# The opening of a fused window-attention and maxout kernel: another order for chunk 0, weights in other pieces, two stores later in a queue

## The chip, the cores and the metric

The kernel runs on one core of a Trainium2 chip. A core has TensorE (matrix products into PSUM, eight banks), VectorE, ScalarE, GpSimd and SyncE, each with an instruction stream of its own, and 16 DMA engines that they share. In the profile's rows these are PE (products) and PEld (their weight loads), DVE, ACT, POOL and SP. The metric is the time of one execution in device microseconds, the median of several runs; lower is better.

## The reference

```
scores = q k^T / 8, of q, k, v: (4 batches, 8 heads, 768 tokens, 64)
keep   = first 4 positions (sinks), or 0 <= token - position < 128
x      = softmax(scores where kept) v, heads side by side: (3072, 512)
h      = max(max(x w1, x w2), x w3)         w1, w2, w3: (512, 768)
out    = h w_out                            w_out: (768, 512), out float32
```

All inputs are float32; the kernel computes its products in bfloat16 with float32 sums.

## The kernel before

The 3072 tokens are cut into 12 chunks of 256, three for each batch, and everything is written out by hand: the kernel is under a manual schedule, each engine takes its instructions in the order of the program's lines, and semaphores make it wait where data or a buffer is not there yet. So the list of calls from line 454 to 660 is the order of each engine's work for chunks 0 to 3; a loop (line 661) does the rest. The change touches that list.

What the calls do, chunk `ci` and (for attention) pair of heads `p` from 0 to 3:

- `load` (line 76) fetches q, k or v of a chunk, 512 KB of float32, on SyncE's queue, whole or in two halves. A `gate` is a one-element write of GpSimd into the target, which holds the load back: `after(wi, c)` (434) copies from column `c` of weight `wi`, and so waits for the piece of the weight that holds the column; `pool_gate` (440) writes a zero.
- `cast_qk` (95) and `cast_v` (104) cast to bfloat16, in halves and quarters, on the engine named. `turn` (109) and `turn2` (129) transpose half of the heads (`g` 0: pairs 0 and 1; `g` 1: pairs 2 and 3) by four TensorE transposes and a copy out of PSUM into `kT` or `qT`. `turn_dma` (150) does it by a DMA transpose for later chunks.
- `premask` (251) begins the score tiles of a pair by a product that writes the mask; `score` (259) adds the scores of the pair. A pair without `premask` is masked after the exponential by `mask` (289) on VectorE. `expo` (282) is two exponentials on ScalarE. `sink_k`, `sink_score`, `sink_v` and `av_open` (224 to 335) are the same for the four sink positions, which chunks 1 and 2 of a batch need. `av` (339) is values times weights, the division and the write into `x_sb`.
- `xpose` (364) transposes the x of half a chunk. `ffn_h(ci, fp, wi)` (383) is a third of the columns (`fp` 0 to 2, 256 each) of x times weight `wi` (0 to 2): eight products of 128 x 256. For weight 0 ScalarE copies the result to `h_sb`, for the others VectorE takes the maximum with what is there. `ffn_y` (406) is half of a chunk's output, six products; `store` (426) writes a chunk out from SyncE's queue.
- `load_w` (234) fetches columns of a weight by a casting DMA issued from GpSimd's queue, float32 to bfloat16, `load_wo` (242) the output weight in two halves.
- `warm` (172) issues products of a zero tile that nothing uses.
- PSUM banks come from a list in order of release (`bank`, `give`, lines 57 to 65): whoever takes a bank waits for its last reader.

The ring of `kT`, `qT`, `vb` has four chunks; raw q, k, v and their casts have two buffers each, y and x two, xT and h three.

Of the kernel before, what the change touches and what calls it, by code (L numbers as in the profile page):

```python
# [16 lines left out]
def kernel(  # L17
# [31 lines left out]
    with tc.manual_schedule():  # L49
# [289 lines left out]
        def av(ci, p):  # L339
# [16 lines left out]
            if p == 0:  # L356
                xs[ci] = work.tile([128, 2, NP, 2, D], BF16, tag="x", bufs=2, name="x_sb")
# [25 lines left out]
        def ffn_h(ci, fp, wi, cuts=1):  # L383
# [12 lines left out]
            if wi == 0:  # L396
                nc.scalar.copy(dst, hp)  # L397
# [8 lines left out]
        def ffn_y(ci, t, eng=None):  # L406
            if t == 0:
                ys[ci] = work.tile([128, 2, d_model], F32, tag="y", bufs=2, name="y_sb")
# [7 lines left out]
        def ffn_y_part(ci, t, c0, c1, eng):  # L416
            if t == 0 and c0 == 0:
                ys[ci] = work.tile([128, 2, d_model], F32, tag="y", bufs=2, name="y_sb")
# [39 lines left out]
        warm(2)  # L458
# [5 lines left out]
        warm(7)  # L464
        cast_qk(0, 'k', 0, nc.vector)
        cast_qk(0, 'k', 1, nc.gpsimd)
        cast_qk(0, 'q', 0, nc.gpsimd)
        premask(0, (0,))
        cast_qk(0, 'q', 1, nc.scalar)
        turn(0, 'k', 0, nc.vector)  # L470
        turn(0, 'k', 1, nc.scalar)
        turn(0, 'q', 1, nc.scalar)
        premask(0, (3,))
        load(1, 'k')
        turn(0, 'q', 0, nc.vector)
        score(0, (0,))
        premask(0, (2,))
        cast_v(0, 0, 0, nc.vector)
        cast_v(0, 1, 0, nc.gpsimd)
        cast_v(0, 1, 1, nc.vector)  # L480
        cast_qk(1, 'k', 0, nc.vector)
        premask(0, (1,))
        load(1, 'q')
        load_w(0, 512, 768)
        load_w(0, 0, 512)
        score(0, (1,))
        score(0, (2,))
        expo(0, 0)
        warm(3)
        sink_k(0)  # L490
        cast_v(0, 0, 1, nc.vector)
        expo(0, 1)
        load_w(1, 512, 768)
        turn2(1, 'k', 0, nc.vector)
        expo(0, 2)
        cast_qk(1, 'k', 1, nc.scalar)
        av_open(0)
        cast_qk(1, 'q', 0, nc.scalar)
        av(0, 0)
        score(0, (3,))  # L500
        sink_v(0)
        cast_qk(1, 'q', 1, nc.gpsimd)
        load_w(1, 0, 512)
        av(0, 1)
        load(1, 'v')
        expo(0, 3)
        turn(1, 'k', 1, nc.scalar)
        turn(1, 'q', 1, nc.vector)
        turn2(1, 'q', 0, nc.vector)
        cast_v(1, 0, 0, nc.gpsimd)  # L510
        cast_v(1, 1, 1, nc.gpsimd)
        cast_v(1, 1, 0, nc.gpsimd)
        cast_v(1, 0, 1, nc.gpsimd)
        premask(1, (0,))
        av(0, 3)
        load(2, 'k', part=0, parts=2, gate=after(0, 300))
        score(1, (0,))
        score(1, (2,))
        av(0, 2)
        load_w(2, 0, 256)  # L520
        load(2, 'k', part=1, parts=2)
        premask(1, (3,))
        score(1, (3,))
        expo(1, 0)
        xpose(0, 0, nc.vector)
# [3 lines left out]
        xpose(0, 1, nc.vector)  # L529
        load_w(2, 256, 512)  # L530
        sink_score(1)
        load_w(2, 512, 768)
        premask(1, (1,))
        score(1, (1,))
        av_open(1)
        cast_qk(2, 'k', 1, nc.gpsimd)
        mask(1, 2)
        expo(1, 3)
        load(2, 'v', gate=after(0, 300))
        expo(1, 1)  # L540
        av(1, 0)
        load(3, 'q', gate=after(2))
        ffn_h(0, 2, 0)
        av(1, 2)
        av(1, 3)
        av(1, 1)
        cast_qk(2, 'k', 0, nc.scalar)
        load(3, 'k')
        ffn_h(0, 0, 0)
        ffn_h(0, 2, 1)  # L550
        ffn_h(0, 1, 0)
        xpose(1, 0, nc.vector)
        xpose(1, 1, nc.vector)
        ffn_h(0, 1, 1)
        ffn_h(1, 0, 0)
        ffn_h(0, 0, 1)
        load_wo()
        factors(msk0, addm0)
        ffn_h(1, 2, 0)
        turn(2, 'k', 0, nc.vector)  # L560
        ffn_h(1, 1, 0)
# [48 lines left out]
        turn(3, 'k', 1, nc.scalar)  # L610
        load(5, 'k', gate=after(0, 300))
        av(2, 1)
        cast_qk(4, 'q', 1, nc.vector)
        turn(3, 'k', 0, nc.scalar)
        ffn_y(1, 0)
        cast_v(3, 1, 1, nc.gpsimd)
        score(3, (1,))
# [198 lines left out]
```

## Time and profile before

| | |
|---|---|
| median of three runs | 178.46 us (178.2 to 179.15) |
| profiled execution | 178.04 us |
| its span in the profile | 176.3 us |
| granted TensorE clock | 0.997 |
| TensorE busy | 169.8 us |
| DMA | 34.90 MB, 31.33 of them on the hardware queue (SyncE), 3.15 on the software queue (GpSimd, weights; counted as written) |

The profile is of one execution. All times are from the start of its span. A row of the timeline has start, length, engine, line of the code, operation and what it writes and reads, and in brackets how long the engine was idle before it and what ended that. A TensorE row's length has the tail of its pipeline in it, so costs are taken from start to start. A row of the DMA view has a queue, its packets, megabytes and share of 16 engines in the stretch asked for (q1 is SyncE's queue, q0 GpSimd's), or a kind of transfer, its size and the time from issue to landing.

### The profile page before, as it was taken

How to read it: one execution, taken by the hardware profiler on the slowest of the kernel's cores; microseconds unless marked ns; L12 is line 12 of the kernel's file. 1: busy time of each engine (PE TensorE's matmuls, PEld its weight loads, DVE VectorE, ACT ScalarE, POOL GpSimd, SP SyncE). 2: the span in 40 equal slices, each digit the busy share in tenths (PEclk: the TensorE clock that was granted, in tenths of full speed). 3: DMA queues.
4: the chain of work that ended last, by engine and by line, in shares of the span. 5: the costliest groups of instructions: out<-in, count | busy, mean ns of one | idle time of the engine just before them, and what ended most of it. 6: DMA issues, size and time to landing. Idle time of an engine off the chain costs nothing.

```text
span 176.3 us, 4635 instructions
## 1 busy us (share of the span) xinstructions
PE 169.8 (96%) x1864; PEld 127.0 (72%) x1877; DVE 120.7 (68%) x262; ACT 86.0 (49%) x172; POOL 66.4 (38%) x126
## 2 busy tenths in 40 slices
PE   7889999999999999999999999999999999999992
PEld 2545999866786697697696796796795795796871
DVE  3387644796697895775775874875785775976451
ACT  4298455758844914914715814814617616420210
POOL 7596507623494693182172054245244000000000
PEclk9999999999999999999999999999999999999998
DMA  5999999999999999987999999999999218203203
GB/s 152 293 283 204 225 226 241 217 295 275 296 244 264 299 188 223 264 186 207 259 192 225 261 177 246 273 139 244 275 164 244 32 29 155 119 4 59 121 0 119
DMA packets 69637, 34.90 MB, mean 198 GB/s; under 512 B 26608, under 2 KB 68080, under 8 KB 69616
## 3 DMA queue, kind: packets, MB, share of 16 engines
q1 hardware_dynamic: 64976, 31.33, 81.1%
q0 software_dynamic: 4496, 3.15, 11.7%
q8 instruction: 14, 0.23, 0.5%
q10 hardware_dynamic: 144, 0.13, 0.2%
q14 instruction: 7, 0.06, 0.1%
HBM read 25.17 MB, written 6.29 MB: 178 GB/s over the span
## 4 chain that ended last, share of the span: by engine, by line
PE 88%; DMA 3%; POOL 3%; DVE 2%; issue 2%; POOLq 0%; SPq 0%; DVEq 0%
PE h_ps L390 52%; PE y_ps L411 17%; PE st L274 6%; PE o L350 6%; DMA v_raw<-in_v_dram 3%; PE pt L115 1%; PE xt L371 1%; DVE h_sb L401 1%; PE o L332 1%; PE sk L300 1%; PE st L256 1%; POOL w L237 1%; PE y_ps L421 1%; DVE e_sb L292 1%; POOL vb L105 0%
## 5 line engine op out<-in xcount | busy, mean ns | idle before, releaser
L390 PE MATMUL h_ps<-xT,w 128*128 128x256 bf16 x864 | 101.3, 273 | 0.1
L390 PEld LDWEIGHTS <-w 128*128 128x128 bf16 x864 | 82.0, 98 | 10.3 <-issue 0.4
L401 DVE TENSOR_TENSOR h_sb<-h_sb,h_ps 128x512 bf16<-128x512 bf16 (+1 forms) x74 | 49.1, 670 | 21.3 <-PE h_ps L390 18.1
L286 ACT ACTIVATE e_sb<-st 128x512 bf16<-128x512 f32 (+1 forms) x96 | 46.5, 577 | 8.0 <-PE st L274 8.0
L397 ACT CAST h_sb<-h_ps 128x512 bf16<-128x512 f32 x36 | 20.9, 585 | 46.9 <-PE h_ps L390 46.7
L105 POOL CAST vb<-v_raw 64x512 bf16<-64x512 f32 x44 | 29.6, 673 | 16.1 <-DMA v_raw<-in_v_dram 11.3
L411 PE MATMUL y_ps<-wo,h_sb 128*128 128x512 bf16 x126 | 31.9, 380 | 0.6
L292 DVE TENSOR_TENSOR e_sb<-e_sb,msk 128x1024 bf16<-128x1024 bf16 (+1 forms) x41 | 26.9, 694 | 0.9 <-ACT e_sb L286 0.8
L101 POOL CAST k_bf<-k_raw 128x512 bf16<-128x512 f32 x18 | 11.9, 679 | 40.5 <-DMA k_raw<-in_k_dram 28.5
L411 PEld LDWEIGHTS <-h_sb 128*128 128x128 bf16 x138 | 12.4, 98 | 14.4 <-issue 1.6
L358 DVE TENSOR_TENSOR x_sb<-o,rc 128x256 bf16<-128x256 f32 x48 | 20.4, 425 | 1.7
L413 DVE COPY y_sb<-y_ps 128x512 f32<-128x512 f32 x13 | 9.0, 692 | 14.2 <-PE y_ps L411 14.1
L350 PE MATMUL o<-vb,e_sb 128*128 128x65 bf16 x352 | 17.0, 194 | 0.3 <-DVE vb L105 0.3
L350 PEld LDWEIGHTS <-e_sb 128*128 128x128 bf16 x352 | 14.7, 97 | 3.0 <-issue 0.5
L274 PE MATMUL st<-qT,kT 64*128 64x128 bf16 (+1 forms) x256 | 14.4, 238 | 0.5 <-DVE qT L119 0.5
L274 PEld LDWEIGHTS <-kT 64*128 64x128 bf16 x256 | 8.4, 94 | 7.6 <-issue 5.7
L101 POOL CAST q_bf<-q_raw 128x512 bf16<-128x512 f32 x17 | 10.1, 618 | 6.9 <-DMA q_raw<-in_q_dram 6.8
L355 DVE RECIPROCAL rc<-o 128x4 f32<-128x4 f32 x48 | 8.5, 177 | 4.6 <-PE o L350 4.4
L306 ACT ACTIVATE e_sink<-sk 128x256 bf16<-128x256 f32 x8 | 3.1, 384 | 14.4 <-PE sk L300 14.4
L413 ACT COPY y_sb<-y_ps 128x512 f32<-128x512 f32 x10 | 5.8, 585 | 3.0 <-PE y_ps L411 2.7
L177 PE MATMUL warm<-wz 128*128 128x512 bf16 x16 | 5.6, 501 | 1.3 <-DVE wz L166 1.2
L237 POOL DMA_DIRECT2D w<-in_moe_w_dram x7 | 5.4, 773 | 0.0
(66 smaller groups left out, 68.8 us busy)
## 6 DMA issues: line engine op xcount, KB each, us to landing
k_raw<-in_k_dram SPq DMA_DIRECT2D x11, 512.0 KB, 5.1
v_raw<-in_v_dram SPq DMA_DIRECT2D x11, 512.0 KB, 7.4
out_dram<-y_sb SPq DMA_DIRECT2D x11, 512.0 KB, 3.2
q_raw<-in_q_dram SPq DMA_DIRECT2D x10, 512.0 KB, 7.3
w<-in_moe_w_dram POOLq DMA_DIRECT2D x5, 256.0 KB, 8.1
q_raw<-in_q_dram SPq DMA_DIRECT2D x4, 256.0 KB, 6.7
w<-in_moe_w_dram POOLq DMA_DIRECT2D x2, 512.0 KB, 8.9
wo<-in_moe_w_out_dram POOLq DMA_DIRECT2D x2, 384.0 KB, 8.1
```

Of the source, the lines that this page charges most:

```text
L101: f(x[:, 2 * g:2 * g + 2].rearrange("q p i a d -> q p a i d"), y[:, 4 * g:4 * g + 4].rearrange("q (p a) i d -> q p a i d", a=2))
L105: eng.tensor_copy(vb[ci % RING][64 * i:64 * i + 64, n, :, 0:D], raws[ci, "v"][64 * n:64 * n + 64, :, i])
L274: nc.tensor.matmul(st[a][:, s:s + q1 - q0].rearrange("q n (i r) -> q n i r", i=2), lhsT=x[hp, n, p].rearrange("q i r -> q (i r)"), rhs=qc[ ...
L286: nc.scalar.activation(e[:, a, lo:], st[a][:, lo:], AF.Exp, scale=scale)
L292: (eng or nc.vector).tensor_mul(e[:, :, lo:], e[:, :, lo:], msk0 if lo else msk)
L350: nc.tensor.matmul(o[:, t, a], lhsT=e[:, a, s], rhs=vb[cv % RING][:, n, 2 * p + a], start=first, stop=True, skip_group_check=True)
L358: nc.vector.tensor_mul(xs[ci][:, :, p], o[:, :, :, 0:D], rc.unsqueeze(3).to_broadcast([128, 2, 2, D]))
L390: nc.tensor.matmul(hp[:, f].rearrange("q (i t r) -> q i t r", i=2, t=2), lhsT=w_sb[wi][:, ds, c0:c0 + 128], rhs=xTs[ci][:, :, ds].rearrang ...
L397: nc.scalar.copy(dst, hp)
L401: nc.vector.tensor_max(dst[:, x], dst[:, x], hp[:, x])
L411: nc.tensor.matmul(yp, lhsT=hs[ci][:, fb, t * 128:(t + 1) * 128], rhs=wo[:, fb], start=(fb == 0), stop=(fb == FB - 1))
L413: (nc.scalar.copy if eng is None else eng.tensor_copy)(ys[ci][:, t], yp)
```

## The change

Nothing is computed in another way, apart from one masking of chunk 1 that moves from `premask` to `mask`. The calls from line 458 to 660 get another order:

- Chunk 0 starts with the second half of the heads: q's half, which is loaded first, is cast, turned and copied first, pairs 2 and 3 are scored first, then 0 and 1. VectorE's casts of v follow its turns at once, and chunk 1's casts of k and q are handed to GpSimd and ScalarE. Warm-up products go from 17 to 9.
- Columns 0 to 512 of weights 0 and 1 are loaded in two pieces of 256 instead of one of 512, all six pieces by GpSimd between its casts. The load of chunk 2's k is gated as before by the piece of weight 0 that holds column 300, which is now columns 256 to 512.
- `ffn_h` of chunk 0 goes in part ahead of chunk 1's value products: weight 0 by columns 512, 256, 0, then weight 1 the same way. The first is copied by VectorE instead of ScalarE (a new argument `eng`).
- The output weight is issued ahead of the load of chunk 3's q, and this load waits for weight 2's column 300 instead of 0.
- For chunk 3, two turns of k, the transposes of chunk 2's x and a `ffn_y` change places with two scores; three casts of v go earlier on GpSimd; `store(0)` and `store(1)` go behind the DMA transposes of chunk 4.
- y has four buffers instead of two; `av` makes its x tile with whichever pair comes first.

```diff
@@ -353,7 +353,7 @@
                         first = False
             rc = work.tile([128, 2, 2], F32, tag="rc", bufs=4, name="rc")
             nc.vector.reciprocal(rc, o[:, :, :, D])
-            if p == 0:
+            if ci not in xs:
                 xs[ci] = work.tile([128, 2, NP, 2, D], BF16, tag="x", bufs=2, name="x_sb")
             nc.vector.tensor_mul(xs[ci][:, :, p], o[:, :, :, 0:D],
                                  rc.unsqueeze(3).to_broadcast([128, 2, 2, D]))
@@ -380,7 +380,7 @@
 
         hs = {}
 
-        def ffn_h(ci, fp, wi, cuts=1):
+        def ffn_h(ci, fp, wi, cuts=1, eng=nc.scalar):
             if ci not in hs:
                 hs[ci] = work.tile([128, FB, 256], BF16, tag="h", bufs=3, name="h_sb")
             hp = bank([128, 2, 256], F32, "h_ps")
@@ -394,7 +394,7 @@
                         start=(ds == 0), stop=(ds == DS - 1))
             dst = hs[ci][:, 2 * fp:2 * fp + 2]
             if wi == 0:
-                nc.scalar.copy(dst, hp)
+                (nc.scalar.copy if eng is nc.scalar else eng.tensor_copy)(dst, hp)
             else:
                 for f in range(cuts):
                     x = slice(2 * f // cuts, 2 * (f + 1) // cuts)
@@ -405,7 +405,7 @@
 
         def ffn_y(ci, t, eng=None):
             if t == 0:
-                ys[ci] = work.tile([128, 2, d_model], F32, tag="y", bufs=2, name="y_sb")
+                ys[ci] = work.tile([128, 2, d_model], F32, tag="y", bufs=4, name="y_sb")
             yp = bank([128, d_model], F32, "y_ps")
             for fb in range(FB):
                 nc.tensor.matmul(yp, lhsT=hs[ci][:, fb, t * 128:(t + 1) * 128], rhs=wo[:, fb],
@@ -415,7 +415,7 @@
 
         def ffn_y_part(ci, t, c0, c1, eng):
             if t == 0 and c0 == 0:
-                ys[ci] = work.tile([128, 2, d_model], F32, tag="y", bufs=2, name="y_sb")
+                ys[ci] = work.tile([128, 2, d_model], F32, tag="y", bufs=4, name="y_sb")
             yp = bank([128, c1 - c0], F32, "y_ps")
             for fb in range(FB):
                 nc.tensor.matmul(yp, lhsT=hs[ci][:, fb, t * 128:(t + 1) * 128],
@@ -455,110 +455,110 @@
         warm(5)
         load(0, 'k')
         load(0, 'q', part=0, parts=2)
-        warm(2)
         load(0, 'v', part=0, parts=2, gate=pool_gate)
         load(0, 'v', part=1, parts=2)
         masks()
         sink_init()
         factors(msk, addm)
-        warm(7)
-        cast_qk(0, 'k', 0, nc.vector)
-        cast_qk(0, 'k', 1, nc.gpsimd)
+        cast_qk(0, 'q', 1, nc.scalar)
+        turn(0, 'q', 1, nc.scalar)
+        premask(0, (2,))
+        warm(4)
+        cast_qk(0, 'k', 1, nc.vector)
+        cast_qk(0, 'k', 0, nc.gpsimd)
         cast_qk(0, 'q', 0, nc.gpsimd)
+        turn(0, 'k', 1, nc.vector)
+        load(1, 'k')
+        premask(0, (3,))
+        turn(0, 'k', 0, nc.scalar)
+        score(0, (2,))
+        score(0, (3,))
+        turn(0, 'q', 0, nc.vector)
         premask(0, (0,))
-        cast_qk(0, 'q', 1, nc.scalar)
-        turn(0, 'k', 0, nc.vector)
-        turn(0, 'k', 1, nc.scalar)
-        turn(0, 'q', 1, nc.scalar)
-        premask(0, (3,))
-        load(1, 'k')
-        turn(0, 'q', 0, nc.vector)
+        load(1, 'q')
+        expo(0, 2)
+        cast_v(0, 1, 0, nc.gpsimd)
+        cast_v(0, 0, 0, nc.vector)
+        cast_v(0, 1, 1, nc.vector)
+        cast_v(0, 0, 1, nc.vector)
+        load_w(0, 512, 768)
+        load(1, 'v')
         score(0, (0,))
-        premask(0, (2,))
-        cast_v(0, 0, 0, nc.vector)
-        cast_v(0, 1, 0, nc.gpsimd)
-        cast_v(0, 1, 1, nc.vector)
-        cast_qk(1, 'k', 0, nc.vector)
+        expo(0, 3)
         premask(0, (1,))
-        load(1, 'q')
-        load_w(0, 512, 768)
-        load_w(0, 0, 512)
         score(0, (1,))
-        score(0, (2,))
         expo(0, 0)
-        warm(3)
+        cast_qk(1, 'k', 0, nc.gpsimd)
+        load_w(0, 256, 512)
+        expo(0, 1)
+        av_open(0)
+        av(0, 2)
+        av(0, 3)
+        turn2(1, 'k', 0, nc.vector)
+        cast_qk(1, 'k', 1, nc.scalar)
+        av(0, 0)
+        cast_qk(1, 'q', 0, nc.gpsimd)
+        cast_qk(1, 'q', 1, nc.scalar)
+        turn(1, 'k', 1, nc.scalar)
+        av(0, 1)
+        premask(1, (0,))
+        premask(1, (1,))
+        turn2(1, 'q', 0, nc.vector)
+        turn(1, 'q', 1, nc.scalar)
         sink_k(0)
-        cast_v(0, 0, 1, nc.vector)
-        expo(0, 1)
+        cast_v(1, 0, 0, nc.vector)
+        cast_v(1, 1, 0, nc.vector)
+        load_w(0, 0, 256)
         load_w(1, 512, 768)
-        turn2(1, 'k', 0, nc.vector)
-        expo(0, 2)
-        cast_qk(1, 'k', 1, nc.scalar)
-        av_open(0)
-        cast_qk(1, 'q', 0, nc.scalar)
-        av(0, 0)
-        score(0, (3,))
+        score(1, (0,))
+        score(1, (1,))
+        expo(1, 0)
+        expo(1, 1)
+        xpose(0, 0, nc.vector)
+        xpose(0, 1, nc.vector)
+        cast_v(1, 1, 1, nc.gpsimd)
+        load_w(1, 256, 512)
+        cast_v(1, 0, 1, nc.gpsimd)
+        load_w(1, 0, 256)
         sink_v(0)
-        cast_qk(1, 'q', 1, nc.gpsimd)
-        load_w(1, 0, 512)
-        av(0, 1)
-        load(1, 'v')
-        expo(0, 3)
-        turn(1, 'k', 1, nc.scalar)
-        turn(1, 'q', 1, nc.vector)
-        turn2(1, 'q', 0, nc.vector)
-        cast_v(1, 0, 0, nc.gpsimd)
-        cast_v(1, 1, 1, nc.gpsimd)
-        cast_v(1, 1, 0, nc.gpsimd)
-        cast_v(1, 0, 1, nc.gpsimd)
-        premask(1, (0,))
-        av(0, 3)
+        sink_score(1)
+        score(1, (3,))
         load(2, 'k', part=0, parts=2, gate=after(0, 300))
-        score(1, (0,))
+        load(2, 'k', part=1, parts=2)
+        ffn_h(0, 2, 0, 1, nc.vector)
+        expo(1, 3)
         score(1, (2,))
-        av(0, 2)
-        load_w(2, 0, 256)
-        load(2, 'k', part=1, parts=2)
-        premask(1, (3,))
-        score(1, (3,))
-        expo(1, 0)
-        xpose(0, 0, nc.vector)
         expo(1, 2)
         load(2, 'q', part=1, parts=2)
         load(2, 'q', part=0, parts=2, gate=pool_gate)
-        xpose(0, 1, nc.vector)
+        load_w(2, 0, 256)
         load_w(2, 256, 512)
-        sink_score(1)
         load_w(2, 512, 768)
-        premask(1, (1,))
-        score(1, (1,))
+        mask(1, 3)
+        ffn_h(0, 1, 0)
+        mask(1, 2)
         av_open(1)
         cast_qk(2, 'k', 1, nc.gpsimd)
-        mask(1, 2)
-        expo(1, 3)
+        av(1, 0)
+        av(1, 1)
+        ffn_h(0, 0, 0)
         load(2, 'v', gate=after(0, 300))
-        expo(1, 1)
-        av(1, 0)
-        load(3, 'q', gate=after(2))
-        ffn_h(0, 2, 0)
+        av(1, 3)
         av(1, 2)
-        av(1, 3)
-        av(1, 1)
+        ffn_h(0, 2, 1)
+        ffn_h(0, 1, 1)
+        xpose(1, 0, nc.vector)
+        xpose(1, 1, nc.scalar)
+        ffn_h(0, 0, 1)
+        ffn_h(1, 2, 0)
         cast_qk(2, 'k', 0, nc.scalar)
+        ffn_h(1, 1, 0)
+        ffn_h(1, 0, 0)
+        load_wo()
+        load(3, 'q', gate=after(2, 300))
         load(3, 'k')
-        ffn_h(0, 0, 0)
-        ffn_h(0, 2, 1)
-        ffn_h(0, 1, 0)
-        xpose(1, 0, nc.vector)
-        xpose(1, 1, nc.vector)
-        ffn_h(0, 1, 1)
-        ffn_h(1, 0, 0)
-        ffn_h(0, 0, 1)
-        load_wo()
         factors(msk0, addm0)
-        ffn_h(1, 2, 0)
         turn(2, 'k', 0, nc.vector)
-        ffn_h(1, 1, 0)
         ffn_h(1, 1, 1)
         turn(2, 'k', 1, nc.scalar)
         cast_v(2, 1, 0, nc.gpsimd)
@@ -607,36 +607,36 @@
         load(5, 'q')
         av(2, 3)
         turn(3, 'q', 1, nc.scalar)
-        turn(3, 'k', 1, nc.scalar)
         load(5, 'k', gate=after(0, 300))
         av(2, 1)
+        ffn_y(1, 0)
+        turn(3, 'k', 1, nc.scalar)
+        turn(3, 'k', 0, nc.scalar)
+        xpose(2, 0, nc.scalar)
+        xpose(2, 1, nc.vector)
+        ffn_y(1, 1)
         cast_qk(4, 'q', 1, nc.vector)
-        turn(3, 'k', 0, nc.scalar)
-        ffn_y(1, 0)
         cast_v(3, 1, 1, nc.gpsimd)
+        cast_v(3, 0, 0, nc.gpsimd)
+        cast_v(3, 0, 1, nc.gpsimd)
         score(3, (1,))
         cast_qk(4, 'q', 0, nc.vector)
         expo(3, 1)
         score(3, (0,))
-        xpose(2, 0, nc.scalar)
-        xpose(2, 1, nc.vector)
-        ffn_y(1, 1)
         cast_qk(4, 'k', 1, nc.gpsimd)
         mask(3, 1)
         cast_v(4, 1, 0, nc.gpsimd)
         ffn_h(2, 0, 0)
         cast_qk(4, 'k', 0, nc.vector)
-        cast_v(3, 0, 0, nc.gpsimd)
         score(3, (3,))
         cast_v(3, 1, 0, nc.vector)
-        store(0)
         turn_dma(4, 'k')
         turn_dma(4, 'q')
+        store(0)
+        store(1)
         score(3, (2,))
-        store(1)
         expo(3, 0)
         expo(3, 3)
-        cast_v(3, 0, 1, nc.gpsimd)
         ffn_h(2, 0, 2)
         mask(3, 0)
         mask(3, 3)
```

## The prediction, made before the changed kernel was run

> **What bounds the kernel now.** First the page: the span, its busy engines, and the slices of TensorE and of the DMA engines.
>
> ```profile
> span 176.3 us, 4635 instructions
> PE 169.8 (96%) x1864; PEld 127.0 (72%) x1877; DVE 120.7 (68%) x262; ACT 86.0 (49%) x172; POOL 66.4 (38%) x126
> ...
> PE   7889999999999999999999999999999999999992
> ...
> DMA  5999999999999999987999999999999218203203
> ```
>
> TensorE is full after its first slices, and so are the DMA engines for three quarters of the span. The waits of TensorE say where it was starved:
>
> ```profile
> PE warm L177 <- DVE wz L166: 1.2, 1, 1.2
> PE st L274 <- DVE qT L119: 0.5, 1, 0.5
> PE o L350 <- DVE vb L105: 0.3, 1, 0.3
> ```
>
> That is all of it, and all in the opening. So the kernel takes a fixed amount of TensorE work plus what the opening loses; any change here shifts TensorE's dense stretch, and the shift lasts to the end unless something stops it again. The timeline of TensorE (start, time, engine, line) has the points at which I measure it:
>
> ```profile
> 8.22 0.34 PE L274 MATMUL st<-qT,kT 64*128 64x256 bf16 x4 [0.52 <-DVE qT L119]
> ...
> 11.26 0.36 PE L350 MATMUL o<-vb,e_sb 128*128 128x65 bf16 x6 [0.28 <-DVE vb L105]
> ...
> 13.34 0.59 PE L256 MATMUL st<-addm,ident 128*128 128x512 bf16 x2
> 13.77 0.35 PE L350 MATMUL o<-vb,e_sb 128*128 128x65 bf16 x6
> ...
> 26.23 1.91 PE L390 MATMUL h_ps<-xT,w 128*128 128x256 bf16 x16
> 27.97 0.39 PE L115 MATMUL pt<-ident,k_bf 128*128 128x128 bf16 x4
> 28.20 1.91 PE L390 MATMUL h_ps<-xT,w 128*128 128x256 bf16 x16
> 29.94 0.39 PE L115 MATMUL pt<-ident,q_bf 128*128 128x128 bf16 x4
> ...
> 31.04 0.39 PE L115 MATMUL pt<-ident,q_bf 128*128 128x128 bf16 x4
> ```
>
> Starts give costs: two products of `ffn_h` take 29.94 - 28.20 = 1.74, so one is 0.87 us; four transposes 28.20 - 27.97 = 0.23; a `premask` pair of chunk 1 13.77 - 13.34 = 0.43. The second thing to see is how little room the last lines have. ScalarE and VectorE cast the q of chunk 2 for the transposes at 29.94 and 31.04:
>
> ```profile
> 28.88 0.62 ACT L101 CAST q_bf<-q_raw 128x512 bf16<-128x512 f32 x1
> ```
> ```profile
> 30.48 0.43 DVE L101 CAST q_bf<-q_raw 128x512 bf16<-128x512 f32 x1 [0.52 <-DMA q_raw<-in_q_dram]
> ```
>
> The VectorE cast waited for its DMA and ended at 30.91; TensorE wanted it at 31.04. **The DMA of chunk 2's q is 0.13 us from being the bound.** The earlier half was cast by 29.50 for 29.94, 0.44 of room. TensorE can be early here only if that data is.
>
> **The change part by part.**
>
> *Chunk 0 (casts, turns, scores, values).* What lands first is unchanged (SyncE's first eight loads stay in order), so k's first copy out of PSUM stays where it is, the first line of VectorE's:
>
> ```profile
> 6.62 0.42 DVE L122 COPY kT<-pt 128x512 bf16<-128x512 bf16 x1 [0.60 <-PE pt L115]
> 7.74 0.42 DVE L119 COPY qT<-pt 128x512 bf16<-128x512 bf16 x1 [0.70 <-PE pt L115]
> 8.39 1.18 DVE L105 CAST vb<-v_raw 64x512 bf16<-64x512 f32 x2 [0.22 <-DMA v_raw<-in_v_dram]
> 10.10 0.43 DVE L101 CAST k_bf<-k_raw 128x512 bf16<-128x512 f32 x1 [0.53 <-DMA k_raw<-in_k_dram]
> 10.55 0.64 DVE L105 CAST vb<-v_raw 64x512 bf16<-64x512 f32 x1
> ```
>
> Before, the first score waited for q's copy, 7.74 + 0.42, and began at 8.22. Now q's second half is turned while k is still on its way, and the first score needs only the copy that ends at 6.62 + 0.42 = 7.04: about 7.1, 1.1 us earlier. Values: the third VectorE cast stood behind the cast of chunk 1's k, which waited 0.53 for its DMA. Now the three go in a row from about 8.46 (after q's copy, at 8.1): 1.18 + 0.64, to about 10.2, as one starts a little before the other ends. So the first value product starts at 10.2 instead of 11.26. The eight warm-up matmuls that go filled waits, and take nothing off the path; what they may have done for the clock is a rival below. The casts handed to GpSimd (k and q of chunk 1) are behind the value products on TensorE, 0.6 to 0.9 us of them beside each other; if that cover fails, the turn of chunk 1's k slips by as much, and q's, which comes later, still sets the place below.
>
> From there I add up TensorE's work. Before, 11.26 to 27.10 (26.23 + 0.87) is 15.84 us, some 0.45 of it pauses before 13.3, so 15.4 of work. After has one `premask` pair of chunk 1 less (-0.43; VectorE has one `mask` more instead), one score of chunk 0 done already (-0.3, the row at 8.22) and the turn of chunk 1's k still to do (+0.23): 14.9. From 10.2 that would end at 25.1. It can't: chunk 1's q lands as before, and its cast, turn and copy have to follow.
>
> ```profile
> 11.92 0.62 ACT L101 CAST q_bf<-q_raw 128x512 bf16<-128x512 f32 x1 [0.16 <-DMA q_raw<-in_q_dram]
> ```
>
> Cast to 12.5, the two `premask` pairs ahead of the turn until 13.0, copy to 13.9; the work there is until then ends at 13.4, so 0.5 is lost, and I allow 0.4 more for scores that wait for PSUM banks. So TensorE stands at the place of 27.10 at about **26.0: 1.1 us early**. The rest hangs on data.
>
> *Weights in thirds.* The DMA queues in chosen stretches (q0 carries weights; packets, MB, share): from 17.0 to 18.0 us a piece of 256 columns, ahead of it, from 14.5 to 16.5, one of 512:
>
> ```profile
> q0 software_dynamic: 372, 0.19, 142.2%
> ```
> ```profile
> q0 software_dynamic: 406, 0.42, 124.3%
> ```
>
> 256 columns go as packets of 512 B: 372 in 1 us, 0.19 MB/us. 512 columns are packets of 1 KB, 0.21 MB/us. A third is 0.262 MB and takes 1.35 us in the one form and 1.26 in the other. Four thirds change from the second to the first (columns 0 to 512 of weights 0 and 1), so **all that comes behind them is about 4 x 0.09 = 0.36 us later**; the engines have no pause in which to make it good (the slices of 9).
>
> GpSimd issued columns 0 to 512 of weight 1 at 12.77, and their landing took:
>
> ```profile
> 12.77 0.74 POOL L237 DMA_DIRECT2D w<-in_moe_w_dram  x1
> ...
> 18.68 0.18 POOL L437 CAST k_raw<-w 1x1 f32<-1x1 bf16 x1 [2.34 <-DMA w<-in_moe_w_dram]
> ...
> 32.05 1.26 POOL L105 CAST vb<-v_raw 64x512 bf16<-64x512 f32 x2 [2.21 <-DMA v_raw<-in_v_dram]
> ```
> ```profile
> w<-in_moe_w_dram POOLq DMA_DIRECT2D x1, 512.0 KB, 9.4
> ```
>
> Seen at 22.2. So its last third is seen at 22.2 + 0.36 = 22.6, the third before it 1.35 sooner, at 21.2. After's TensorE starts its first product of `ffn_h` at about 15.9 (q's copy 13.9, two scores, eight transposes, two copies of 0.42 and what stands between), and four products (3.5), a score (0.3) and sink and value products (1.2) later, at 20.9, it wants the second of these, at 22.4 the last. Waits of 0.2 to 0.3 make 26.0 into 26.3: 22.6 and four products and a turn, 3.7.
>
> *GpSimd's queue and chunk 2.* GpSimd's issues now stand between casts. Its four casts of v stood ahead of the gate for chunk 2's k (L437, 18.68), and the gate then waited 2.34 for weight 0; now four issues of 0.74 and two casts of 0.6, from 13.05 on, end at about 17.3, and the piece it waits for is there by then. So k and q of chunk 2 and weight 2 are asked for 1.4 us earlier. Does that bring them earlier? The queues in three stretches (20.75 to 21.5, 21.75 to 22.25, 25 to 28):
>
> ```profile
> q1 hardware_dynamic: 425, 0.21, 94.3%
> q0 software_dynamic: 48, 0.03, 26.1%
> ```
> ```profile
> q0 software_dynamic: 175, 0.09, 133.2%
> q1 hardware_dynamic: 20, 0.01, 7.4%
> ```
> ```profile
> q0 software_dynamic: 641, 0.32, 76.8%
> q1 hardware_dynamic: 655, 0.33, 53.2%
> ```
>
> All had been asked for by 21.05, yet first k ran almost alone, then weight 2 almost alone: whole transfers in the order of their requests, mixed only where requests overlapped. That order does not change (all of weights 0 and 1 ahead, then k, weight 2 and q interleaved by the same offsets within 0.1). So an earlier request buys nothing: q comes when the bytes ahead of it have passed, 0.36 later. Its last cast moves from 30.48 to 30.8, ends at 31.3, and the turn at 31.04 is at **31.3**. I take +0.3. Bounds: -0.1 (the thirds cost nothing; TensorE still waits at 30.96) and, downward, -0.9 if the data came as early as it is asked for. The 0.9 to 1.1 gained is idle time at 29 to 31 us, and the opening could be 0.7 worse without being noticed.
>
> *Later edits.* The gate for chunk 3's q now waits for weight 2's second piece, with the output weight issued ahead of it. Queued behind it on GpSimd are `factors` and the v casts at 32.05, which wait 2.21 for their own data: room for both. On the DMA queue the output weight and q change places. Turns of chunk 3's k move behind one `ffn_y`, and two scores behind another; `mask(3, 1)` then waits for an exponential and blocks VectorE's casts behind it:
>
> ```profile
> 44.14 1.46 PE L411 MATMUL y_ps<-wo,h_sb 128*128 128x512 bf16 x6
> ```
> ```profile
> 48.00 0.69 DVE L401 TENSOR_TENSOR h_sb<-h_sb,h_ps 128x512 bf16<-128x512 bf16 x1 [1.32 <-PE h_ps L390]
> ```
>
> The score moves behind such an `ffn_y` (1.46 with its tail) and eight transposes (0.45), the mask with it by up to 1.9; VectorE's 1.32 of idle time covers all but 0.6. Cost 0 to 0.6; I take 0, the end that the idle row is nearest to, because the casts that now come after the mask stood right before that idle time. The stores moved behind transposes on SyncE's queue let those run first; nobody on this core waits for a store, and the y tiles have four buffers now. 0.
>
> **Sum:** +0.3 on the span of 176.3, whose profiled execution took 178.04 (1.74 around the span); that run is 0.42 under the median, 178.46. So 178.46 + 0.3 = **178.8**.
>
> **The rivals.**
>
> *Slower: chunk 2's loads share with weight 1 (179.4).* Asked for at 17.5, k could run from about 18.8 if the engines alternate. By the stretch from 20.75, weight 1 was through at 20.75 (seen 1.45 later), after 21.1; at 18.8 it has 2.3 us x 0.19 = 0.44 MB to go, and the mixed stretch gives q0 0.32 MB in 3 us, 0.107 per us: 4.1 us, to 22.9, seen at 24.35. Four products and a turn follow, to 28.05 where it was 27.10: +0.95. It decides when the last piece is seen after 23.5. The alternating stretches speak against it, the mixed one for it. The Trainium skill's page "DMA: Bandwidth & Descriptors", section "Queues, rings and completion order", says that each engine goes round-robin between the queue rows at packet granularity; by that rule this rival is the forecast. The stretches with 94% and 26%, 133% and 7% disagree, the one at 77% and 53% agrees. Chance 0.16.
>
> *Slower: the clock comes late (179.4).* Warm-up matmuls (L177) from 1.2 to 4.5 us and from 4.5 to 5.7:
>
> ```profile
> 1.20:4.50 3.30, 3.30 (x8) 1.16 (x9) 1.00 0.75 211
> 4.50:5.70 1.20, 1.20 (x7) 0.49 (x5) 1.00 1.20 297
> ```
>
> Eight in 3.3 us, then seven in 1.2: TensorE runs at half speed until 4.5. After has only five, to 3.4, and a pause until 4.4. One further stretch of 3.3 at half speed, to 7.8, puts the opening about 1.3 later (the transposes, masks and warm-ups from 4.4 take 2.8 us instead of 1.4) and hides under q's wait; two, with the scores at half speed as well, put it about 2.0 later: TensorE is then at the turn of 29.94 at 31, +0.9. The Trainium skill's "TensorE: Matmul & The Clock Gate", Part 1, has the full clock after a busy window of 3.4 us that runs free of the kernel; the 3.3 here agrees, and whether a window with a pause counts no run here shows. Chance 0.09.
>
> *Faster: q keeps up (177.5).* If an earlier request does move k and q ahead of weight 2, TensorE keeps 0.8 to 1.1: 177.4 to 177.7. The mixed stretch leaves room for it. Chance 0.20, two thirds of it under -0.5%.
>
> **How the numbers follow.** Forecast 0.55 (178.4 to 179.3, most of the middle's 0.6 in it). About 0.5%, 0.9 us, is what a measurement of this kernel can tell from no change. Faster 0.13; slower 0.25, both rivals just past the bound; same 0.62. Range 177.4 to 179.9: both sides' cases, and 0.4 for the spread of runs (178.2 to 179.15) above.
>
> **What would show it.** Right: first score near 7.1, first value product near 10.2, first `ffn_h` near 16, then a wait of TensorE of 0.4 to 1 us on q's cast at 29 to 31. Wrong: no such wait and the turn before 30.7 (the third rival), a wait on weight 1 over 0.8 (the first), or warm-up matmuls of 0.43 us after 4.6 (the second). My weakest step is that the queues serve whole transfers in order.

## The result, and the profile after

| | before | changed |
|---|---|---|
| median | 178.2 us (177.85 to 179.15, 22 runs) | 179.1 us (178.25 to 180.37, 22 runs) |
| ratio, 95% interval | | 1.0051 [1.0037, 1.0066] |
| profiled execution | 178.04 us, span 176.3 | 178.26 us, span 176.5 |

The change made the kernel 0.9 us slower, inside the range, with the sign of the forecast and three times its size (+0.3). The profiled execution of the changed kernel is one of its two fastest, 0.84 us under its median. So most of the loss is not in this profile; it is looked for below in other executions. Medians here are of all executions, ratios and intervals of the undisturbed ones, and only in f4 below do the two differ.

The page of the changed kernel, the rows that answer to those of before:

```profile
span 176.5 us, 4618 instructions
PE 168.6 (96%) x1855; PEld 126.5 (72%) x1867; DVE 120.5 (68%) x263; ACT 86.4 (49%) x173; POOL 66.2 (38%) x127
...
PE   5978999999999999999999999999999999999992
...
DMA  5999999999999999997998999999999215203203
```

TensorE's first slices are emptier than before, and its busy time is 1.2 us less, with eight warm-ups and one `premask` pair fewer. Its waits:

```profile
PE warm L177 <- DVE wz L166: 1.2, 1, 1.2
PE pt L115 <- ACT q_bf L101: 0.9, 1, 0.9
PE o L350 <- DVE vb L105: 0.9, 1, 0.9
PE st L274 <- DVE qT L141: 0.4, 1, 0.4
PE st L274 <- DVE qT L119: 0.2, 1, 0.2
```

All are in the opening again. The timeline of TensorE at the points of the prediction (start, time, engine, line):

```profile
1.20 2.32 PE L177 MATMUL warm<-wz 128*128 128x512 bf16 x5 [1.20 <-DVE wz L166]
4.45 0.61 PE L115 MATMUL pt<-ident,q_bf 128*128 128x128 bf16 x4 [0.94 <-ACT q_bf L101]
...
5.50 1.91 PE L177 MATMUL warm<-wz 128*128 128x512 bf16 x4
7.20 0.63 PE L115 MATMUL pt<-ident,k_bf 128*128 128x128 bf16 x4
...
8.54 0.50 PE L274 MATMUL st<-qT,kT 64*128 64x256 bf16 x8
...
11.82 0.53 PE L350 MATMUL o<-vb,e_sb 128*128 128x65 bf16 x12 [0.90 <-DVE vb L105]
...
17.25 1.03 PE L390 MATMUL h_ps<-xT,w 128*128 128x256 bf16 x8
...
30.39 0.39 PE L115 MATMUL pt<-ident,q_bf 128*128 128x128 bf16 x4
...
31.48 0.39 PE L115 MATMUL pt<-ident,q_bf 128*128 128x128 bf16 x4
```

The four warm-ups from 5.50 take 0.43 us each (1.70 until 7.20), half speed: the full clock is not there at 4.5 but one stretch later. (The profile's column of the granted clock reads 1.00 there all the same; the half speed is read from the lengths.) That is the second rival's sign. The first turn of k is at 7.20 instead of 6.19, the first score at 8.54 instead of 8.22, the first value product at 11.82 instead of 11.26. `ffn_h` begins at 17.25, before 17.85, and the turn that was at 31.04 is 0.44 later. The data it needs, on VectorE:

```profile
30.82 0.43 DVE L101 CAST q_bf<-q_raw 128x512 bf16<-128x512 f32 x1 [0.35 <-DMA q_raw<-in_q_dram]
```

The forecast had 30.8. TensorE does not wait for it here, as the forecast said it would: it is late itself, in part through the slow clock.

Chunk 2's k was asked for at 17.41 by SyncE. The DMA queues from 17.5 to 20.5 us (queue, packets, MB, share):

```profile
q0 software_dynamic: 1100, 0.55, 139.1%
q8 instruction: 1, 0.02, 2.0%
```

Not one packet of SyncE's queue in these 3 us: k waits until weight 1 has passed. Whole transfers in the order of their requests, as the prediction took it. The Trainium skill's rule ("DMA: Bandwidth & Descriptors", "Queues, rings and completion order"), an engine going round-robin between queue rows packet by packet, is not what these 3 us show. From 22 to 25 us both queues move, 0.36 MB of weight 2 and 0.27 MB on SyncE's queue; these had been asked for at the same time.

### The profile page after: what moved, and what is told of

It is laid out like the page before. It is cut to its first block, busy times and chain, and to the rows that moved or that the text cites. A ratio compares the mean times of both kernels' runs of the same rounds, so it can differ in the third digit from the quotient of the medians.

```text
span 176.5 us, 4618 instructions
## 1 busy us (share of the span) xinstructions
PE 168.6 (96%) x1855; PEld 126.5 (72%) x1867; DVE 120.5 (68%) x263; ACT 86.4 (49%) x173; POOL 66.2 (38%) x127
## 4 chain that ended last, share of the span: by engine, by line
PE 85%; DVE 8%; ACT 2%; issue 2%; DMA 2%
PE h_ps L390 49%; PE y_ps L411 17%; PE o L350 6%; PE st L274 6%; DVE h_sb L401 2%; PE pt L115 2%; DVE x_sb L358 2%; DMA q_raw<-in_q_dram 2%; ACT e_sb L286 1%; DVE vb L105 1%; PE o L332 1%; PE warm L177 1%; DVE e_sb L292 1%; PE xt L371 1%; PE y_ps L421 1%
## 5 line engine op out<-in xcount | busy, mean ns | idle before, releaser
L105 POOL CAST vb<-v_raw 64x512 bf16<-64x512 f32 x42 | 27.2, 647 | 19.3 <-DMA v_raw<-in_v_dram 17.9
L237 POOL DMA_DIRECT2D w<-in_moe_w_dram x9 | 7.0, 786 | 0.0
L177 PE MATMUL warm<-wz 128*128 128x512 bf16 x9 | 4.2, 631 | 1.2 <-DVE wz L166 1.2
```

The source lines that it names most:

```text
L105: eng.tensor_copy(vb[ci % RING][64 * i:64 * i + 64, n, :, 0:D], raws[ci, "v"][64 * n:64 * n + 64, :, i])
```

## The experiments

Each kernel is the changed one or the one before with parts exchanged, timed against the kernel before on the same chip. I name the parts: the opening (order of chunks 0 and 1, warm-ups, places of the weights), the thirds, the gate of chunk 3's q, the later edits (chunk 3's turns, masks, stores, y buffers).

**First four: is it the clock?** The theory was that the late clock costs the median what the profile hides.

```diff
e1: -warm(5)   +warm(7)                      (pause ahead of the first turn filled)
e2: -load_w(0, 256, 512) ... -load_w(0, 0, 256)   +load_w(0, 0, 512)     (weight 1 likewise)
e3: before, with -load_w(0, 0, 512)  +load_w(0, 256, 512) +load_w(0, 0, 256)   (weight 1 likewise)
e4: before, with the order of the changed kernel from turn(3, 'q', 1) on, y: bufs=4
```

> The changed kernel with seven warm-up products ahead of q's turn instead of five: at half speed (0.43 us each) they fill the pause of TensorE from 3.4 to 4.4 us and nothing else moves. Clock theory: without the pause the full clock comes by 4.6 to 5 us in most executions, as in the kernel before; the first score goes from 8.5 to about 7.1 us, TensorE gets to the turn of q's second half about 1 us earlier, meets the late q there, and the median falls by 0.4 to 0.9 us to 178.2 to 178.7 with less spread. Theory that the weights' pieces alone cost the 0.9: no change, 179.1.

> The changed kernel with columns 0 to 512 of weights 0 and 1 in one piece again (packets of 1 KB). Theory of the pieces: what lies behind them on the DMA queues lands 0.36 us earlier, the cast of q's first half starts at about 30.5 instead of 30.82, and if q is the bound the median falls by 0.3; but weight 1's columns are seen 1.3 us later as one piece. Clock theory: TensorE comes to q late anyway, so the time stays within 0.2 us of 179.1, or rises by what TensorE waits for weight 0's and 1's whole pieces (0 to 0.6).

> The kernel before with weights 0 and 1 in thirds and nothing else. Theory of the pieces: q lands 0.36 us later with only 0.13 us of room, TensorE waits, +0.2 to +0.3 us on 178.2. If the 512 B packets cost nothing: 0. Clock theory: 0 from the clock, since the warm-up products are those of before.

> The kernel before with the late edits alone: order of chunk 3's turns, transposes, scores and value casts, the two stores behind the DMA transposes, y in four buffers. The two profiles have TensorE 0.44 us late ahead of this stretch and 0.25 us behind it, so it would be -0.2 us; the prediction had 0 to +0.6. If the 0.9 came from here: +0.5 or more.

| kernel | median | ratio, 95% interval |
|---|---|---|
| e1, warm-ups filled | 179.24 | 1.0044 [1.0019, 1.0070] |
| e2, thirds undone | 179.30 | 1.0051 [1.0023, 1.0079] |
| e3, thirds alone | 178.77 | 1.0026 [1.0007, 1.0045] |
| e4, later edits alone | 178.27 | 0.9986 [0.9966, 1.0006] |

The clock theory fell. In e1 the four warm-ups after the first turn run at full speed, 1.03 us for all, and the first score comes at 7.71, yet the kernel is as slow. The pause does decide the clock: in all seven traces of kernels with five warm-ups these four take 1.82 to 1.91 us, in all three with seven (e1, and f4 and i1 below) 1.03. The timeline of e1 shows where the gain went; VectorE and TensorE at 31 us, then TensorE at 70:

```profile
31.47 0.43 DVE L101 CAST q_bf<-q_raw 128x512 bf16<-128x512 f32 x1 [1.39 <-DMA q_raw<-in_q_dram]
```
```profile
31.95 0.40 PE L115 MATMUL pt<-ident,q_bf 128*128 128x128 bf16 x4 [0.39 <-DVE q_bf L101]
...
65.96 3.66 PE L390 MATMUL h_ps<-xT,w 128*128 128x256 bf16 x32
70.72 0.29 PE L300 MATMUL sk<-qT,ks 128*32 128x256 bf16 x4 [1.09 <-DMA qT<-q_bf]
```

The first is the predicted wait for chunk 2's q. The second is new: `sink_score` of chunk 5 waits for chunk 5's q, which a DMA transpose delivers. In e1 it is issued at 66.18, before at 63.76; SyncE and TensorE of the kernel before, with the transpose's time to landing:

```profile
63.76 1.26 SPq L154 DMA_TRANSPOSE qT<-q_bf  x1
```
```profile
DMA to landing us min/median/max: 5.0/5.0/5.0
```
```profile
68.87 0.29 PE L300 MATMUL sk<-qT,ks 128*32 128x256 bf16 x4
```

63.76 + 5.0 = 68.8, TensorE needs it at 68.87. **So there was a second place where DMA data arrived just in time, 40 us behind the one that I had found.**

The thirds cost 0.46 us by themselves (e3, 0.0026 x 178.4), and taking them out of the change gained nothing that shows (e2). The forecast had 0.36 for them, but e3's trace has another cause than packets. GpSimd of the kernel before, then of e3, then TensorE of e3:

```profile
9.23 1.71 POOL L237 DMA_DIRECT2D w<-in_moe_w_dram  x2
...
12.22 0.61 POOL L101 CAST q_bf<-q_raw 128x512 bf16<-128x512 f32 x1
```
```profile
9.49 2.46 POOL L237 DMA_DIRECT2D w<-in_moe_w_dram  x3
...
13.17 0.61 POOL L101 CAST q_bf<-q_raw 128x512 bf16<-128x512 f32 x1
```
```profile
13.84 0.40 PE L115 MATMUL pt<-ident,q_bf 128*128 128x128 bf16 x4 [0.76 <-POOL q_bf L101]
```

One more piece is one more issue on GpSimd, 0.75 us, ahead of its cast of chunk 1's q, and TensorE waits 0.76 for that cast. TensorE is 0.96 late from there (12.88 in the kernel before) and still 0.95 late at the turn of chunk 2's q, which does not wait for its data. In the changed kernel this cast waits 0.46 for its own data, so the issue does not hold it up there.

**Four more: which part makes the stream late?** The next theory, G, put it on the new gate of chunk 3's q; rival O on the opening.

```diff
f1: -load_wo() -load(3, 'q', gate=after(2, 300)) -load(3, 'k')   +the three at their old places
f2: before, with the new opening; weights in pieces of 512 and 256, the rest as before
f3: before, with load_wo() ahead and load(3, 'q', gate=after(2, 300))
f4: e1, e2 and f1 together
```

> The changed kernel with one part undone: chunk 3's q waits again for weight 2's first columns and is asked for ahead of the output weight, as before; all else as changed. Theory G (the new wait of chunk 3's q makes q, k and v of chunk 3 and every load behind them 1 to 2 us later, until TensorE waits at about 70 us for the DMA transpose of chunk 5's q, 0.9 to 1.3 us): chunk 3's q is issued before 28.5 us, no such wait of sink_score at 70 us, and the median falls from 179.1 to 178.2 to 178.6, what the thirds add less what the later edits gain. Rival O (the opening itself costs it, by its order of loads and its clock): the median stays at 178.9 to 179.3.

> The kernel before with the new opening alone: order of chunks 0 and 1, warm-ups, weights 0 and 1 issued at the new places but in pieces of 256 and 512 columns as before; the gate of chunk 3's q, the order for chunk 3, the stores and y's buffers as before. Theory G: within 0.3 of before, 178.1 to 178.6, since TensorE waits for chunk 2's q with or without an early opening. Rival O: 178.9 to 179.4, and chunk 4's and 5's transposes 0.5 to 1.5 us later than before (47.0 and 58.4 us).

> The kernel before with one part alone: the output weight issued ahead of chunk 3's q, and this q waiting for weight 2's column 300. Theory G: 178.9 to 179.3, q of chunk 3 issued 1 to 2 us later than 27.62, and a wait of TensorE of 0.5 to 1.3 us at 65 to 75 us. Rival O: within 0.2 of before, 178.2 to 178.5.

> The changed kernel with three parts undone: seven warm-ups ahead of the first loads instead of five, weights 0 and 1 in pieces of 256 and 512 columns, chunk 3's q as before. What is left is the new order of chunk 0 and the later edits. Theory G: 177.8 to 178.3, the gain of the later edits, with full clock from 4.5 us and TensorE waiting 0.4 to 1 us for chunk 2's q at 29 to 31. Rival O: still 178.8 to 179.3.

| kernel | median | ratio, 95% interval |
|---|---|---|
| f1, gate undone | 179.67 | 1.0066 [1.0045, 1.0087] |
| f2, opening alone | 178.83 | 1.0010 [0.9983, 1.0037] |
| f3, gate alone | 178.72 | 1.0001 [0.9979, 1.0022] |
| f4, warm-ups, thirds and gate undone | 179.49 | 1.0045 [1.0021, 1.0070] |

G fell: the gate costs nothing alone, and undoing it helps nothing. f1 shows both waits again, for chunk 2's q and for chunk 5's:

```profile
30.68 0.40 PE L115 MATMUL pt<-ident,q_bf 128*128 128x128 bf16 x4 [0.52 <-ACT q_bf L101]
...
32.30 0.40 PE L115 MATMUL pt<-ident,q_bf 128*128 128x128 bf16 x4 [0.35 <-DVE q_bf L101]
...
70.47 0.29 PE L300 MATMUL sk<-qT,ks 128*32 128x256 bf16 x4 [0.50 <-DMA qT<-q_bf]
```

**Three more: is it the stores?** e1, e2 and f1 have the later edits and the wait at 70; f2, without them, has none. In e1 and e2 the DMA engines moved 227 and 206 GB/s from 44 to 54 us, before 279. Theory S: the stores behind chunk 4's transposes leave the engines dry.

```diff
h1: +store(0)   turn_dma(4, 'k')  turn_dma(4, 'q')   -store(0) -store(1)   score(3, (2,))   +store(1)
h2: +cast_qk(4, 'k', 0, nc.vector)   mask(3, 1) ...   -cast_qk(4, 'k', 0, nc.vector)
h3: everything from turn(2, 'k', 1, nc.scalar) on as before, y: bufs=2
```

> The changed kernel with the two stores back at their old places: chunk 0's ahead of the DMA transposes of chunk 4, chunk 1's one score later; all else as changed. Theory S (with the stores behind the transposes, the DMA engines run dry at 49 to 53 us while the transposes wait; the loads behind them end about 1 us later, and TensorE waits 0.7 to 1.3 us at 70 us for the transpose of chunk 5's q): no such wait, the engines' mean in 44 to 54 us back from 206 to 217 GB/s to over 250, and a median of 178.3 to 178.8. Rival O (the opening's lateness, clock and thirds cost it whatever the stores do): 178.9 to 179.5, with the wait at 70 us still there.

> The changed kernel with VectorE's cast of chunk 4's k ahead of mask(3, 1), so that the transposes of chunk 4 no longer wait for a mask; the stores stay behind them. Theory S as I hold it: the transposes are issued at 46.5 to 47 instead of 47.9 to 48.7, half or more of the wait at 70 us goes, and the median is 178.4 to 178.9. If only the stores matter: 179.0 to 179.4, the wait as before. Rival O: 178.9 to 179.5.

> The changed kernel with everything from the second turn of chunk 2's k on as before (turns and transposes for chunk 3, casts of v, stores, two y buffers): the new opening, the thirds and the gate of chunk 3's q are left. Theory S: 178.5 to 178.9, what the thirds and the opening add by themselves, with no wait at 70 us. Rival O: 179.0 to 179.5, at least as slow as the whole change.

| kernel | median | ratio, 95% interval |
|---|---|---|
| h1, stores back | 179.17 | 1.0038 [1.0013, 1.0062] |
| h2, cast ahead of the mask | 179.34 | 1.0047 [1.0022, 1.0072] |
| h3, later edits undone | 179.74 | 1.0072 [1.0046, 1.0099] |

S fell too: without any later edit (h3) the kernel is as slow or slower, and TensorE still waits 0.2 at 70 us. In h1 the engines are back at 268 GB/s from 44 to 54 us, and the median is not. h2 does not test S: its transposes of chunk 4 are issued at 47.92, those of the changed kernel at 47.88. h1 happens to show the second rival in full. From 8.39 to 10.5 its TensorE is still at half speed (0.63 for four transposes, where the full clock gives 0.39):

```profile
8.39 0.63 PE L115 MATMUL pt<-ident,k_bf 128*128 128x128 bf16 x4
...
9.71 0.61 PE L115 MATMUL pt<-ident,q_bf 128*128 128x128 bf16 x4
```

Its turns of chunk 2's q are at 31.17 and 32.27, 1.23 late, and the rival had priced that at +0.9. There is no wait at 70: chunk 5's q has landed at 67.8, 2.3 us ahead of its reader.

**One more: chunk 2's q ahead of weight 2.** Does TensorE keep the opening's gain if q comes early?

```diff
i1: e1 and e2, and
-load_w(2, 0, 256) -load_w(2, 256, 512) -load_w(2, 512, 768)
 cast_qk(2, 'k', 1, nc.gpsimd)
+load_w(2, 256, 512) +load_w(2, 0, 256) +load_w(2, 512, 768)
```

> The changed kernel with seven warm-ups ahead of the first loads, weights 0 and 1 in pieces of 256 and 512 columns as before, and weight 2 issued behind the first cast of chunk 2's k, so that both halves of chunk 2's q are asked for ahead of it. Theory D (two places bind on DMA data: chunk 2's q at 31 us and the transposed q of chunk 5 at 70 us, which waits until the whole stream of loads ahead of it has passed): the last cast of chunk 2's q starts before 29.8 instead of 30.8 to 31.8, the first ffn_y at 36.4 to 37.2 (before 37.4, changed 37.8), but TensorE then waits 0.5 to 2 us for chunk 5's transposed q at 70, and the median is 178.0 to 178.8, no real gain. Rival Q (chunk 2's q alone took the opening's gain): no wait over 0.3 at 70 us and 177.1 to 177.8. Rival O (the opening costs by itself, with q or without): 178.9 to 179.5, and the first ffn_y at 37.6 or later.

It took 183.81 us, 1.0299 [1.0259, 1.0339]; every theory missed. TensorE waited 1.3 us for weight 0 at 18.8, so it was at the turns of q no sooner than the changed kernel, and whether it keeps a gain was not answered. The rest came from weight 2 and the output weight passing almost alone. The queues from 24 to 32 us of i1, then of the kernel before:

```profile
q0 software_dynamic: 1615, 0.83, 82.5%
q1 hardware_dynamic: 751, 0.37, 17.0%
```
```profile
q0 software_dynamic: 1196, 0.72, 62.2%
q1 hardware_dynamic: 2187, 1.09, 57.4%
```

The v of chunk 2, asked for at 27.07, stood behind them, and its casts on GpSimd waited until 38.07; the last two of them ended at 41.85, and TensorE waited for them until 41.90 (GpSimd's rows, then TensorE's):

```profile
38.07 1.63 POOL L105 CAST vb<-v_raw 64x512 bf16<-64x512 f32 x2 [7.31 <-DMA v_raw<-in_v_dram]
...
40.23 1.62 POOL L105 CAST vb<-v_raw 64x512 bf16<-64x512 f32 x2
```
```profile
41.90 0.37 PE L350 MATMUL o<-vb,e_sb 128*128 128x65 bf16 x7 [2.36 <-POOL vb L105]
```

**What the twelve give together.** From `sink_score` of chunk 5 to TensorE's last row it is 102.5 us in the kernel before, the changed one and the ten variants of the next table, which leaves out f4 and i1, whose clock falls to half on the way (before 68.87 to 171.37, e1 70.72 to 173.21, all within 0.01). So all of the difference is made ahead of 71 us, and one start measures it:

| kernel | second turn of chunk 2's q | chunk 5's q landed | `sink_score` of chunk 5 | its wait |
|---|---|---|---|---|
| before | 31.04 | 68.8 | 68.87 | none |
| f3 gate alone | 32.17 | 67.1 | 69.62 | none |
| e3 thirds alone | 31.99 | 67.3 | 69.71 | none |
| e4 later edits alone | 31.64 | 69.3 | 69.30 | none |
| changed | 31.48 | 67.4 | 69.07 | none |
| f2 opening alone | 31.54 | 67.7 | 69.45 | none |
| h1 | 32.27 | 67.8 | 70.02 | none |
| e2 | 31.54 | 70.0 | 70.07 | 0.74 |
| h2 | 32.46 | 70.3 | 70.29 | 0.35 |
| f1 | 32.30 | 70.5 | 70.47 | 0.50 |
| h3 | 31.79 | 70.5 | 70.55 | 0.16 |
| e1 | 31.95 | 70.7 | 70.72 | 1.09 |

The four with the old opening have 31.71 and 69.38 as means, the eight with the new one 31.92 and 70.08: 0.2 is lost by the turn, and another 0.5 between there and 70 us, 0.36 of it the waits of the last column. One execution each, spread over 0.8 us with the old opening and 1.7 with the new: this says where, not how much. Nor is the second place tight each time: without a wait the data came 0.1 us or less ahead of its reader in before and e4, but 1.6 to 2.5 us ahead in the changed kernel, f2, f3, e3 and h1. How much comes from the medians. One number for each part, fitted by least squares to the ratios of the changed kernel, e1 to e4, f1 to f4 and h3, each weighted by its interval, gives (with the standard error) **opening +0.38% (0.09), thirds +0.24% (0.07)**, gate 0.00% (0.07), later edits -0.05% (0.08), the two warm-ups +0.01% (0.11). In us: 0.67, 0.43, 0, -0.1, 0; the sum is 1.0, measured 0.9. The worst fit is the opening alone, which measured 0.10% where the sum wants 0.38%. So the sizes lean on the assumption that parts add, and **the medians do not decide whether they do**. Without the two kernels that have the opening or the thirds alone (f2, e3), the same fit gives the opening +0.71% (0.15) and the thirds +0.04% (0.12). The four parts measured alone (f2, e3, f3, e4: 0.10, 0.26, 0.01, -0.14) add up to 0.23% (0.23), and together they measured 0.51% (0.07).

A combination that costs something is seen in the DMA queues from 16 to 24 us (before; thirds alone, e3; changed):

```profile
q0 software_dynamic: 1862, 1.26, 105.5%
q1 hardware_dynamic: 1006, 0.50, 22.6%
```
```profile
q0 software_dynamic: 2521, 1.25, 116.0%
q1 hardware_dynamic: 975, 0.49, 22.4%
```
```profile
q0 software_dynamic: 2509, 1.25, 116.7%
q1 hardware_dynamic: 759, 0.38, 19.4%
```

The weights' 1.25 MB cost 11 points of 16 engines more as 512 B packets. In e3 SyncE's queue moves as much as before all the same; in the changed kernel it has 0.12 MB less. At the rate of the whole stretch (1.63 MB in 8 us) that is 0.6 us for what comes behind. Both queues together move 1.72 to 1.76 MB in the four kernels with the old opening, 1.70 and 1.71 in the two with the new one and whole pieces (f2, e2), and 1.42 to 1.63 in the six with the new opening and thirds: the stream falls behind where the two meet. The last cast of chunk 2's q starts at 31.10, 31.06 and 31.43 in the mean of the three groups, which differ less than their members (30.48 to 31.98).

## Why the prediction was right, and where it was short

- **First score 7.1, first value product 10.2, first `ffn_h` 16: late by 0.6 to 0.9 even without the clock.** e1 has 7.71, 10.86 and 16.85, the changed kernel 8.54, 11.82 and 17.25. k's first copy did not stay at 6.62: it was at 7.22 in e1, where k was cast only at 6.31 (before 5.59), and at 7.87 in the changed kernel, through the clock.
- **The clock.** The second rival's first stretch came, as the row of warm-ups at 0.43 shows, and filling the pause (e1) moved the median by nothing that the intervals show, as it would if it hides in the wait for q. h1's execution had more of it, at the price of the second stretch. TensorE busy for 2.3 to 2.4 of the 3.3 us from 1.2 to 4.5 did not bring the full clock in any of seven traces; 3.1 to 3.3 us did in the other seven. The Trainium skill's "TensorE: Matmul & The Clock Gate", Part 1, has it come after a window of sustained work, at a phase that varies between runs of one kernel; the row of the changed kernel and those of h1, whose opening is the same, agree.
- **Thirds, 0.36 us: the size is near, the mechanism is not shown, and e3's agreement is luck.** Alone they cost 0.46, but in e3's trace that comes from one more issue on GpSimd, and TensorE did not wait for chunk 2's q. Removed from the change they give back nothing (e2). What fits the forecast is that in the new opening q's last cast is 0.4 later with thirds than with whole pieces, as means of six and two executions. (The forecast's 1.35 us for a piece was also short: 0.262 / 0.19 is 1.38, which makes the term 0.48.)
- **Order of the queues: right.** Nothing of k moved while weight 1 was on its way, although it was asked for 1.4 us earlier. The first rival falls with that, and so does the third.
- **Chunk 2's q as the place where the gain ends: right as a place.** In e1, f1, h2 and h3 TensorE waited there, 0.35 to 0.43 for the last cast, and so it did in f3 with the old opening (0.68). In the changed kernel's own trace it did not. That the cast came at 30.82 as forecast is luck in part: with the loads in the order of before it starts anywhere from 30.48 to 31.69.
- **Later edits, taken at 0 of 0 to 0.6: right.** -0.05% (0.08) by the fit. `mask(3, 1)` did wait, 1.60 us for its exponential, and e4's median shows no cost of it.
- **The step that fell short: "the opening could be 0.7 worse without being noticed".** It made chunk 2's q the last thing that DMA data could hold up, and put the shift at 31.04 through to the end. The runs show a second such place, chunk 5's transposed q at 70 us, with 0.1 us of room in the profile before; of the seven executions of variants with the new opening five waited there, 0.16 to 1.09. In the changed kernel's profiled execution, one of its fastest, the room was 1.6, so that this place is what its median pays is likely and not shown. The term for the opening was 0; alone it measured +0.18 us with 0 in the interval, and beside the other parts +0.67 by the fit. So the range held, but the sum found a third of the loss. The profile's page had a hint: DMA engines at 9 for three quarters of the span. I checked the room only where the moved instructions read.

What stays open: whether the parts add or a combination of them costs the rest, and how the loss divides between the two places, since each trace is one execution, and q's last cast, waiting for its DMA, was at 30.48 in before and at 31.69 in f3, where all that is asked for ahead of it is the same; and why the opening alone measured 0.10%. That the thirds removed from the change gained nothing (e2) is within the intervals; whole pieces have a price of their own in f4 and i1, where TensorE waits 1.9 and 1.3 us for weight 0, but not in e2's trace. A version that beats both kernels was not found: the later edits alone (e4) come nearest, 0.9986 with 1 in the interval.

## What to carry to other kernels

Where TensorE and the DMA engines are both full, look for every place where DMA data arrives just in time, far behind the change too: compare each transfer's landing with the start of its first reader. Time gained ahead of such a place can be lost there, as in e1. Read in a variant's trace what makes it slow, even where its time comes out as expected: the thirds alone cost about what was forecast, and in the trace it was an issue on another engine. Compare the sum of the parts timed alone with the whole. Loads that move little when alone (the casting queue of i1) are better put between loads of the other queue than in a row of their own.

## What the runs showed of the hardware that was not expected

- After TensorE's wait of 2.4 us at 41.9 in i1 its clock went to half for a stretch (busy, clock granted, DMA share, GB/s in windows of TensorE alone):

```profile
39.50:42.30 2.80, 0.44 (x10) 1.00 0.58 139
42.40:45.80 3.40, 3.40 (x27) 0.50 0.87 250
46.00:50.00 4.00, 3.95 (x44) 1.00 1.20 296
```

  In that execution the wait cost its own length and, at half speed, about half of 3.4 us more (an estimate from these rows). f4's profiled execution has the same behind a wait of 1.9 us at 19.80: granted clock 0.50 from 21.4 to 24.4. The wait of 1.3 us at 18.76 in i1 was not followed by it.
- The casting queue alone moved 0.55 MB in 3 us (changed, 17.5 to 20.5); with SyncE's queue beside it the engines moved 1.81 MB in 8 us of before (24 to 32) and 1.20 in the same stretch of i1, where it was nearly alone.
- The DMA transpose of chunk 5's q landed 3.1 to 3.2 us after its issue in five of the twelve traces of the table and 4.5 to 5.0 in the other seven.
- A load's landing varies by as much as any part of this change is worth: k of chunk 0, with the same loads ahead of it in all fourteen traces, is cast at 5.54 (changed) to 6.43 (f4), in before at 5.59.
